# Linear attention, kv and M computed head by head on 32-column and 32x32 tiles of TensorE

## The chip, the cores and the metric

The kernel runs on one core of one Trainium2 chip. The metric is the device time of one execution in microseconds. The kernel before takes 298.92 us, the median of three runs (298.63 to 299.31).

## The reference

Two branches share one input x of 2048 rows by 640 columns and are mixed by a gate:

```python
qkv = (x @ wqkv).reshape(B, S, 3, H, Dh)      # H = 32 heads, Dh = 20
phi = lambda t: jnp.where(t > 0, t + 1, jnp.exp(t)) + 1e-6
pq, pk = phi(q), phi(k)
kv = einsum("bhsd,bhse->bhde", pk, v)          # per head 20 x 20
z = einsum("bhsd->bhd", pk)
o = (pq @ kv) / (pq . z + 1e-6)                # per head
b = o.reshape(B, S, D) @ wo
return g * a + (1 - g) * b                     # a: an SSM convolution of x; g: sigmoid of x . gate_w
```

Everything is float32.

## The kernel before

The k rows are made first, 128 at a time, and with them G = x^T phi(k), a 640 by 640 sum in PSUM (the long part of the program, until about 145 us). G is copied to SBUF as GT, in five blocks b of 128 rows. Since v = x Wv, a head's kv is a product of 20 columns of Wv with the same 20 columns of GT, summed over b. M is kv times wo, head by head, 640 by 640. The output is then phi(q), scaled by 1/den, times M. This last stage (fp, from about 200 us on) reads M as two float32r parts, a rounded high part and the remainder, Mh and Ml, and does three products for each float32 one (`mm3`, lines 105 to 108). kv and M are plain float32 products; the trace shows two matmuls for each of them. With a `tile_position` (row, column) a product uses only a part of the 128 by 128 array.

From 145 us on the order of the work is set by a list, `PLAN` (line 64): each word calls one function, which issues its instructions on all engines, and each engine runs its instructions in that order. `q` is one q block (15 matmuls of 512 columns, exponential and relu on ACT, the rest of phi and the accumulator of den on DVE), `z` the constants and the gate row, `kv`, `m` the products in question, `c` one convolution block, `d` den's two matmuls and the reciprocal, `ml` the reload of M, `n` the scaling of one q block, `y` a finished convolution block, `f` one output block.

The heads are taken in six groups of 120 columns (`GRP`, the last of 40), each in two parts of 60 columns, three heads. `kv_mm(pr)` does two groups: for each part and b a product 60 by 60 into PSUM (line 279), of which `bdm` (ones in three 20 by 20 blocks) keeps the blocks of the three heads (line 284). `m_mm(pr)` multiplies the two groups' kv with wo. Its four parts lie on the four 64x64 tiles of the array (line 297), in two halves of 320 columns. ACT then rounds each PSUM bank into Mgh (`hi`, line 100) and DVE subtracts it into Mgl (`lo`, line 103). Both are stored to DRAM (line 315), from where `m_load` (line 706) reads them in the order of rows that the last stage wants.

PSUM after 145 us is eight banks in three rings: m of two, f of three, q of three. A ring's next tile waits until the work on the one that it replaces is done. An insertion of M takes two tiles of m and two of f. SBUF tiles are rings too: `bufs` is their length, `st` and `wo` hold what was loaded, `m1` holds GT and later Mh, `m2` holds Wv and later Ml.

Of the kernel before, what the change touches and what calls it, by code (L numbers as in the profile page):

```python
# [30 lines left out]
F32 = mybir.dt.float32  # L31
# [17 lines left out]
GRP = [(i * 120, min(120, D - i * 120)) for i in range(6)]  # L49
HC = 60  # L50
# [14 lines left out]
q0 z kv0 kv1 kv2 q0 q0 m0 q0 c q0 m1  # L65
q1 d0 q1 m2 ml n0 q1 n0 n0 q1 n0 y q1 n0
# [8 lines left out]
def f32(ap):  # L75
    return ap.bitcast(F32)


def body(tc, i, outT):
# [19 lines left out]
    def hi(dst, src):  # L99
        act.activation(dst, src, AF.Copy)  # L100
# [9 lines left out]
    def col(tag, n=NB, dt=F32):  # L110
        return pc.tile([P, n], dt, tag=tag, name=tag)
# [27 lines left out]
    bdm = col("bdm", HC)  # L139
    kvz = [col(f"kvT{k}", P) for k in range(3)]  # L140
# [7 lines left out]
    gap = col("gap", 16)  # L148
# [3 lines left out]
    M_d = [dram.tile([D, D], F32, name=f"M_d{x}") for x in "hl"]  # L152
# [101 lines left out]
    kvs, wos = {}, {}  # L254


    def parts(gi):
        c0, n = GRP[gi]
        return [(r, c0 + o, min(HC, n - o)) for r, o in ((0, 0), (64, HC)) if o < n]

    def wo_load(gi):
        tag, nb = ("st", 3) if gi in (0, 1, 2) else ("wo", 2)
        w = wos[gi] = pw.tile([P, D + 2], F32, tag=tag, bufs=nb, name="wo")
        for r, c, n in parts(gi):
            m = min(64, D - c) if r == 0 else n
            sp.dma_start(w[r : r + m, :D], i["wo"][c : c + m, :])
# [3 lines left out]
    def out_row(gi, r):  # L270
        return r if gi % 2 == 0 else 64 - r

    def kv_mm(pr):
        p = pqp.tile([P, 512], F32, tag="f", bufs=3, name="kvps")
        kvT = kvs[pr] = kvz[pr]
        for k, gi in enumerate((2 * pr, 2 * pr + 1)):
            for b in range(NB):
                for r, c, n in parts(gi):
                    pe.matmul(p[r : r + n, k * 64 : k * 64 + n], Wv[:, b, c : c + n], GT[:, b, c : c + n],
                              start=(b == 0), stop=(b == NB - 1))  # L280
        for k, gi in enumerate((2 * pr, 2 * pr + 1)):
            for r, c, n in parts(gi):
                o = out_row(gi, r)
                dve.tensor_tensor(kvT[r : r + n, o : o + n], p[r : r + n, k * 64 : k * 64 + n], bdm[r : r + n, :n],
                                  op=OP.mult)

    def m_mm(pr):
        kvT = kvs.pop(pr)
        both = 2 * pr, 2 * pr + 1
        ps = {}  # L290
        for hf in range(2):
            for gi in both:
                ps[gi, hf] = mbank("mps") if hf == 0 else pqp.tile([P, 512], F32, tag="f", bufs=3, name="mps")
            for gi in both:
                for r, c, n in parts(gi):
                    o = out_row(gi, r)
                    pe.matmul(ps[gi, hf][o : o + 64, :320], kvT[r : r + n, o : o + 64],
                              wos[gi][r : r + n, hf * 320 : hf * 320 + 320], start=True, stop=True,
                              tile_position=(r, o))
        for gi in both:  # L300
            wos.pop(gi)
        if pr == 1:
            wo_load(NB)
        for gi in both:
            rows = slice(0 if len(parts(gi)) == 2 else out_row(gi, 0), P)
            h = pq.tile([P, D], F32R, tag="so", bufs=2, name="Mgh")
            l = pw.tile([P, D + 2], F32R, tag="st", bufs=3, name="Mgl")
            for hf in range(2):
                sl = slice(hf * 320, hf * 320 + 320)
                hi(h[rows, sl], ps[gi, hf][rows, :320])  # L310
                lo(l[rows, sl], ps[gi, hf][rows, :320], h[rows, sl])
            for v, to in ((h, M_d[0]), (l, M_d[1])):
                for r, c, m in parts(gi):
                    o = out_row(gi, r)
                    sp.dma_start(to[c : c + m, :], f32(v[o : o + m, :D]))
# [204 lines left out]
    for r in (0, 64):  # L520
        sp.dma_start(bdm[r : r + HC, :], i["bdm"][:HC, :HC])
# [18 lines left out]
    for T in range(1, NT):  # L540
# [56 lines left out]
        if T == NT - 1:  # L597
            wqA, wqB = w_tiles(3 * P, "wA", "wqA"), w_tiles(CB, "wB", "wqB")
            for c in WQ:
                wq_split(wqA, c, 0, 3)  # L600
            for c in WQ:
                wq_split(wqB, c, 3, NB)
                raw.pop(c)
            gates()
            for gi in range(NB):
                wo_load(gi)
# [17 lines left out]
    def mbank(name):  # L624
        return pqp.tile([P, 512], F32, tag="m", bufs=2, name=name)
# [73 lines left out]
    def m_load():  # L699

        for x, tag, src in zip("hl", ("m1", "m2"), M_d):
            w = pc.tile([P, NB, D], F32, tag=tag, name="M" + x)
            m[x] = w.bitcast(F32R)
            rows = src.rearrange("(h b i) c -> b h i c", b=NB, i=QI)
            for b in range(NB):
                sp.dma_start(w[:, b, :], rows[b])
# [29 lines left out]
    for w in PLAN.split():  # L736
# [12 lines left out]
        elif what == "kv":  # L749
            kv_mm(k)  # L750
        elif what == "m":
# [193 lines left out]
```

## Time and profile before

| | us |
|---|---|
| median of 3 runs (lowest, highest) | 298.92 (298.63, 299.31) |
| the profiled execution | 298.69 |
| its span | 296.9 |
| TensorE busy in the span | 291.7 |
| DVE, ACT, POOL busy | 228.6, 125.1, 47.0 |
| kv products, start to the next q matmul | 150.29 to 153.56 |
| the three insertions of M start at | 160.56, 168.82, 177.56 |
| loads of Mh and Ml are issued | 186.65 to 193.35 |
| first output product | 199.78 |

A row of the timeline gives the start, the duration of the merged instructions, the engine, the line, the operation, out<-in, partitions by elements and the count; what stands in brackets is the idle time before it and what ended it. PE rows are matmuls, PEld rows loads of weights. For matmuls the shape is rows times columns of the array, then the moving operand. Ends of matmuls are modelled, so a distance between starts is safer than a duration.

### The profile page before, as it was taken

The numbers are of one execution on the slowest core, as the hardware profiler recorded it, in microseconds if no ns is written. First come the engines' busy times: TensorE is split into PE (matmuls) and PEld (weight loads), VectorE is DVE, ScalarE is ACT, GpSimd is POOL, SyncE is SP. The second block draws the span as 40 slices with busy tenths as digits, with TensorE's granted clock in tenths as the row PEclk, the third lists the DMA queues.
The fourth block names the chain that finished last, engine by engine and source line by source line (L and its number), as shares of the span: only waits on it lengthen the run. The fifth ranks groups of instructions, "written<-read, shape, count | busy, mean of one in ns | idle before, by whom it ended". The sixth has DMA issues, their size and how long they took to land.

```text
span 296.9 us, 4579 instructions
## 1 busy us (share of the span) xinstructions
PE 291.7 (98%) x1627; PEld 254.3 (86%) x1627; DVE 228.6 (77%) x355; ACT 125.1 (42%) x262; POOL 47.0 (16%) x52
## 2 busy tenths in 40 slices
PE   8999999999999999999999999999999999999994
PEld 7998899999999999999887777888888888888884
DVE  2869987899999799955743769968683777787992
ACT  3555144653565545337624374562323233314100
POOL 3601760000000000000000000003313203232541
PEclk9999999999999999999999999999999999999999
DMA  6925477257767854280364563792416022426323
GB/s 171 330 69 184 132 242 232 86 200 234 235 152 256 249 168 156 82 256 1 88 174 138 164 203 106 231 329 79 141 35 186 29 71 71 142 73 182 125 85 111
DMA packets 28409, 46.00 MB, mean 155 GB/s; under 512 B 3771, under 2 KB 10827, under 8 KB 28383
## 3 DMA queue, kind: packets, MB, share of 16 engines
q1 hardware_dynamic: 28383, 45.66, 49.0%
q8 instruction: 15, 0.25, 0.3%
q14 instruction: 11, 0.09, 0.1%
HBM read 32.92 MB, written 12.72 MB: 154 GB/s over the span
## 4 chain that ended last, share of the span: by engine, by line
PE 96%; DMA 1%; SPq 0%; ACT 0%; DVE 0%; issue 0%
PE qp L106 8%; PE fp L107 8%; PE fp L108 8%; PE fp L106 8%; PE qp L107 8%; PE qp L108 8%; PE g L232 6%; PE g L231 6%; PE g L234 6%; PE k L108 6%; PE k L107 6%; PE k L106 6%; PE g L459 3%; PE r L247 2%; PE r L246 2%; PE r L245 2%
## 5 line engine op out<-in xcount | busy, mean ns | idle before, releaser
L444 POOL TENSOR_TENSOR yb<-yb,gb 128x512 f32<-128x512 f32 x20 | 28.3, 1417 | 217.8 <-DMA yb<-y_d 199.6
L108 PE MATMUL fp<-pTl,Mh 128*128 128x512 f32 (+1 forms) x105 | 39.8, 379 | 0.0
L107 PE MATMUL fp<-pTh,Ml 128*128 128x512 f32 (+1 forms) x105 | 39.8, 379 | 0.0
L106 PE MATMUL fp<-pTh,Mh 128*128 128x512 f32 (+1 forms) x105 | 39.8, 379 | 0.0
L232 PE MATMUL g<-ph,xl 128*128 128x512 f32 x80 | 31.4, 392 | 0.0
L231 PE MATMUL g<-ph,xh 128*128 128x512 f32 x80 | 31.3, 391 | 0.0
L652 DVE SCALAR_TENSOR_TENSOR qe<-qe,qr 128x512 f32<-128x512 f32 x20 | 14.3, 716 | 21.7 <-ACT qr L649 21.6
L100 ACT ACTIVATE pTh<-qe 128x512 fp32r<-128x512 f32 x20 | 12.6, 633 | 41.4 <-DVE qe L688 41.4
L210 DVE SCALAR_TENSOR_TENSOR e<-e,r 128x320 f32<-128x320 f32 x32 | 15.7, 496 | 13.2 <-ACT e L207 13.2
L106 PE MATMUL qp<-xTh,wqAh 128*128 128x512 f32 x60 | 23.8, 396 | 0.0
L648 ACT ACTIVATE qe<-qp 128x512 f32<-128x512 f32 x20 | 11.9, 595 | 28.0 <-PE qp L108 23.0
L204 ACT ACTIVATE e<-k 128x320 f32<-128x320 f32 x12 | 5.3, 438 | 43.4 <-PE k L108 43.4
L107 PE MATMUL qp<-xTh,wqAl 128*128 128x512 f32 x60 | 23.4, 390 | 0.0
L108 PE MATMUL qp<-xTl,wqAh 128*128 128x512 f32 x60 | 23.4, 389 | 0.0
L234 PE MATMUL g<-pl,xh 128*128 128x512 f32 x80 | 23.3, 389 | 0.0
L106 PEld LDWEIGHTS fp<-pTh,Mh 128*128 128x128 f32 x105 | 19.8, 188 | 3.8
L107 PEld LDWEIGHTS fp<-pTh,Ml 128*128 128x128 f32 x105 | 19.7, 188 | 3.8
L108 PEld LDWEIGHTS fp<-pTl,Mh 128*128 128x128 f32 x105 | 19.7, 188 | 3.7
L103 DVE TENSOR_TENSOR pTl<-qe,pTh 128x512 fp32r<-128x512 f32 x20 | 16.1, 817 | 6.8 <-ACT pTh L100 6.3
L424 DVE TENSOR_TENSOR_SCAN y<-y,cY,zero 128x512 f32<-128x512 f32 x16 | 20.5, 1278 | 0.8 <-ACT y L423 0.8
L108 PE MATMUL k<-wkBl,xTh 128*128 128x320 f32 x60 | 18.5, 309 | 0.0
L107 PE MATMUL k<-wkBh,xTl 128*128 128x320 f32 x60 | 18.5, 309 | 0.0
(171 smaller groups left out, 720.9 us busy)
## 6 DMA issues: line engine op xcount, KB each, us to landing
xraw<-in_x SPq DMA_DIRECT2D x16, 320.0 KB, 4.4
u<-in_xT SPq DMA_DIRECT2D x20, 256.0 KB, 5.7
out_T<-o SPq DMA_DIRECT2D x19, 256.0 KB, 2.6
y_d<-y SPq DMA_DIRECT2D x16, 256.0 KB, 2.4
yb<-y_d SPq DMA_DIRECT2D x16, 256.0 KB, 3.1
xTraw<-in_xTt SPq DMA_DIRECT2D x12, 320.0 KB, 4.5
Wv<-in_wv SPq DMA_DIRECT2D x5, 320.0 KB, 5.8
Mh<-M_dh SPq DMA_DIRECT2D x5, 320.0 KB, 4.5
```

What stands on the lines that cost most here:

```text
L100: act.activation(dst, src, AF.Copy)
L103: (eng or dve).tensor_tensor(dst, src, f32(h), op=OP.subtract)
L106: pe.matmul(out, ah, bh, start=start, stop=False)
L107: pe.matmul(out, al, bh, start=False, stop=False)
L108: pe.matmul(out, ah, bl, start=False, stop=stop)
L210: dve.scalar_tensor_tensor(e, e, 1.0, r[:, :n], op0=OP.min, op1=OP.add)
L231: pe.matmul(gps[b], xh[:, s], h[:, :512], start=t == 0, stop=False)
L232: pe.matmul(gps[b], xl[:, s], h[:, :512], start=False, stop=False)
L234: pe.matmul(gps[b], xh[:, b * P : b * P + P], l[:, :512], start=False, stop=t == NT - 1)
L424: dve.tensor_tensor_scan(y, y, zero.to_broadcast([P, 512]), cY[:, c], op0=OP.add, op1=OP.add)
L444: pool.tensor_tensor(ys[j], ys[j], gbs[j // NB], op=OP.mult)
L652: dve.scalar_tensor_tensor(e, e, 1.0, r, op0=OP.min, op1=OP.add)
```

## The change

The heads are taken one by one. Head 16 s + 4 r + c stands in set s (0 or 1), row r and column c of four. A kv product takes 32 columns of Wv (20 of the head, 12 that are not used) against the head's 20 columns of GT, on the tile (0, 32 r) of 128 rows by 32 columns; `kv_mm(s)` makes sixteen heads, 80 products. Two copies move the blocks to `kvT`; the mask `bdm` with its two loads is gone. `m_mm(n)` is set n/2 and half n mod 2 of M: sixteen products, each on its own 32x32 tile, one PSUM bank for each r. The 32 rows of a head keep their 12 rows of padding: M in DRAM has 1024 rows instead of 640, stored in half rows of 320 columns, by five stores for each insertion: four of 128 rows and one of 512. `m_load` leaves the padding out. The second set's wo is loaded into GT's place once kv is done. The list is changed: two kv words instead of three, directly followed as before by a q block, and four m words, after the q blocks 2, 3, 5 and 6, instead of three, after 3, 5 and 7.

```diff
 PLAN = """
-q0 z kv0 kv1 kv2 q0 q0 m0 q0 c q0 m1
-q1 d0 q1 m2 ml n0 q1 n0 n0 q1 n0 y q1 n0
+q0 z kv0 kv1 q0 m0 q0 m1 q0 c q0 m2
+q1 m3 d0 q1 ml n0 q1 n0 n0 q1 n0 y q1 n0
...
-    bdm = col("bdm", HC)
-    kvz = [col(f"kvT{k}", P) for k in range(3)]
+    kvz = [col(f"kvT{k}", P) for k in range(2)]
...
-    M_d = [dram.tile([D, D], F32, name=f"M_d{x}") for x in "hl"]
+    M_d = [dram.tile([32 * H, D], F32, name=f"M_d{x}") for x in "hl"]
...
+    def wo_load(s):
+        if s == 0:
+            v = [pw.tile([P, D + 2], F32, tag=t, bufs=n, name="wo") for t, n in (("st", 3), ("wo", 2)) for _ in range(2)]
+        else:
+            w = pc.tile([P, NB, D], F32, tag="m1", name="wo1")
+            v = [w[:, c, :] for c in range(4)]
+        wos[s] = v
+        wo = i["wo"]
+        for c in range(4):
+            row = (16 * s + c) * DH
+            n = 4 if row + 12 * DH + 32 <= D else 3
+            src = bass.AP(tensor=wo.tensor, offset=wo.offset + row * D, ap=[[4 * DH * D, n], [D, 32], [1, D]])
+            sp.dma_start(v[c][: n * 32, :D], src)
+            if n == 3:
+                sp.dma_start(v[c][96 : 96 + DH, :D], wo[row + 12 * DH : row + 13 * DH, :])
+
+    def kv_mm(s):
         p = pqp.tile([P, 512], F32, tag="f", bufs=3, name="kvps")
...
+        for c in range(4):
             for b in range(NB):
...
+                for r in range(4):
+                    h0 = (16 * s + 4 * r + c) * DH
+                    n = min(32, D - h0)
+                    pe.matmul(p[32 * r : 32 * r + n, 32 * c : 32 * c + DH], Wv[:, b, h0 : h0 + n],
+                              GT[:, b, h0 : h0 + DH], start=(b == 0), stop=(b == NB - 1), tile_position=(0, 32 * r))
+        src, dst = [v[:, :P].rearrange("p (c q) -> p c q", q=32)[:, :, :DH] for v in (p, kvz[s])]
+        for c, rows in ((slice(0, 3), P), (slice(3, 4), 96 + DH)):
+            dve.tensor_copy(dst[:rows, c, :], src[:rows, c, :])
+
+    Mg = {}
+
+    def m_mm(n):
+        s, hf = divmod(n, 2)
+        sl = slice(hf * 320, hf * 320 + 320)
+        ps = [mbank("mps") if r < 2 else pqp.tile([P, 512], F32, tag="f", bufs=3, name="mps") for r in range(4)]
+        for c in range(4):
+            for r in range(4):
+                pe.matmul(ps[r][32 * c : 32 * c + 32, :320], kvz[s][32 * r : 32 * r + DH, 32 * c : 32 * c + 32],
+                          wos[s][c][32 * r : 32 * r + DH, sl], start=True, stop=True, tile_position=(32 * r, 32 * c))
+        if hf == 0:
+            big = pc.tile([P, NB, D], F32R, tag="m2", name="Mg")
+            v = [pw.tile([P, D + 2], F32R, tag=t, bufs=nb, name="Mgs")
+                 for t, nb in ((("st", 3),) if s == 0 else (("st", 3), ("st", 3), ("wo", 2), ("wo", 2)))]
+            if s == 0:
+                v += [pq.tile([P, D], F32R, tag="so", bufs=2, name="Mgs") for _ in range(2)] + [big[:, 4, :]]
+            Mg[s] = big, v
+        big, v = Mg[s]
+        for r, p in enumerate(ps):
+            h, l = (big[:, r, sl], v[r][:, sl])[:: 1 - 2 * s]
+            hi(h, p[:, :320])
+            lo(l, p[:, :320], h)
+        for r in range(4):
+            row = 512 * s + P * r
+            sp.dma_start(M_d[1 - s][row : row + P, sl], f32(v[r][:, sl]))
+        rows = M_d[s][512 * s : 512 * s + 512, sl]
+        sp.dma_start(rows.rearrange("(r p) n -> p r n", p=P), f32(big[:, :4, sl]))
...
-            rows = src.rearrange("(h b i) c -> b h i c", b=NB, i=QI)
+            rows = src.rearrange("(h q) c -> h q c", q=32)
             for b in range(NB):
-                sp.dma_start(w[:, b, :], rows[b])
+                sp.dma_start(w[:, b, :], rows[:, b * QI : b * QI + QI, :])
...
         elif what == "kv":
             kv_mm(k)
+            if k == 1:
+                wo_load(1)
```

TensorE around the kv products, before (kvps is their PSUM tile, gp the gate row, qp a q block):

```order
L347 MATMUL cp<-zsl,bm 128x2
L326 MATMUL gp<-ident,g 16x128
L279 MATMUL kvps<-GT,Wv 60x60 x50
L279 MATMUL kvps<-GT,Wv 40x40 x5
L106 MATMUL qp<-xTh_131,wqAh 128x512
```

and now (the last head has no columns behind it, so its five products are 20 by 20):

```order
L342 MATMUL cp<-zsl,bm 128x2
L321 MATMUL gp<-ident,g 16x128
L278 MATMUL kvps<-GT,Wv 32x20 x143
L278 MATMUL kvps<-GT,Wv 20x20
L278 MATMUL kvps<-GT,Wv 32x20 x3
L278 MATMUL kvps<-GT,Wv 20x20
...
L104 MATMUL qp<-xTh_128,wqAh 128x512
```

160 products stand where 55 stood, in the same place.

TensorE between the sixth q block and den's products (dp), where the last insertion now is, with the engines whose semaphores each row waits for:

```order
L106 MATMUL qp<-xTl_462,wqAh 128x512
L292 MATMUL mps<-wo_1969,kvT_100 32x320 [waits DVE_49] x2
L292 MATMUL mps<-wo_1969,kvT_100 32x320
L292 MATMUL mps<-wo_1969,kvT_100 32x320 [waits DVE_49]
L292 MATMUL mps<-wo_1969,kvT_100 32x320 x12
L665 MATMUL dp<-acch,bm 128x512 [waits DVE_49]
```

Before, den's products followed the q block directly and the last insertion came one q block later. The first, second and fourth product of this insertion wait for DVE, and twelve stand behind.

DVE from the fourth q block to the reciprocal, before (Mgl is M's remainder, qe and acc are q blocks' work, y the convolution):

```order
L652 SCALAR_TENSOR_TENSOR qe<-qe,qr 128x512
L658 SCALAR_TENSOR_TENSOR acc<-qe,zc,acc 128x512
L424 SCALAR_TENSOR_TENSOR y<-y,cY,zero 128x512
L427 SCALAR_TENSOR_TENSOR y<-u,dsk,y 128x512
L652 SCALAR_TENSOR_TENSOR qe<-qe,qr 128x512
L658 SCALAR_TENSOR_TENSOR acc<-qe,zc,acc 128x512
L103 TENSOR_TENSOR accl<-acc,acch 128x512
L103 TENSOR_TENSOR Mgl<-mps,Mgh 128x320 x4
L652 SCALAR_TENSOR_TENSOR qe<-qe,qr 128x512
L677 RECIPROCAL d<-d 128x512
```

and now:

```order
L419 SCALAR_TENSOR_TENSOR y<-y,cY,zero 128x512
L422 SCALAR_TENSOR_TENSOR y<-u,dsk,y 128x512
L644 SCALAR_TENSOR_TENSOR qe<-qe,qr 128x512
L650 SCALAR_TENSOR_TENSOR acc<-qe,zc,acc 128x512
L101 TENSOR_TENSOR accl<-acc,acch 128x512
L101 TENSOR_TENSOR Mg<-mps,Mgs 128x320 x4
L644 SCALAR_TENSOR_TENSOR qe<-qe,qr 128x512
L101 TENSOR_TENSOR Mg<-mps,Mgs 128x320 x4
L669 RECIPROCAL d<-d 128x512
```

Four more subtractions, the last insertion's, stand ahead of the reciprocal; before they stood behind it.

More of the change, by code (lines that the diff above doesn't have):

```diff
@@ L48 @@
 CA, CB = 320, 320
-GRP = [(i * 120, min(120, D - i * 120)) for i in range(6)]
-HC = 60
 EPS = 1e-6
@@ L147, in body @@
     bm, zh = col("bm", P, F32R), col("zh", H)
-    gap = col("gap", 16)
+    gap = col("gap", 76)
     pool.memset(gap, 0.0)
@@ L251, in g_out @@
         (hi if eng is act else dve.tensor_copy)(GT[:, b, :512], src)
[L254 to L266, printed above, removed]
@@ L270, in out_row @@
-    def out_row(gi, r):
-        return r if gi % 2 == 0 else 64 - r
-    def kv_mm(pr):
+    wos = {}
+    def wo_load(s):
[13 more added lines that the diff above has]
+                sp.dma_start(v[c][96 : 96 + DH, :D], wo[row + 12 * DH : row + 13 * DH, :])
@@ L274, in kv_mm @@
+    def kv_mm(s):
         p = pqp.tile([P, 512], F32, tag="f", bufs=3, name="kvps")
-        kvT = kvs[pr] = kvz[pr]
-        for k, gi in enumerate((2 * pr, 2 * pr + 1)):
+        for c in range(4):
             for b in range(NB):
[L278 to L315, printed above, removed]
@@ L519, in body @@
     sp.dma_start(ident, i["ident"])
-    for r in (0, 64):
-        sp.dma_start(bdm[r : r + HC, :], i["bdm"][:HC, :HC])
     sp.dma_start(dtc, i["log_dt"])
@@ L604, in body @@
             gates()
-            for gi in range(NB):
-                wo_load(gi)
+            wo_load(0)
     g_rest(NT - 1)
```

## The prediction

> **What bounds the kernel now.** I read the page first, then the waits, then the timeline of TensorE around the work that the change touches.
>
> ```profile
> span 296.9 us, 4579 instructions
> PE 291.7 (98%) x1627; PEld 254.3 (86%) x1627; DVE 228.6 (77%) x355; ACT 125.1 (42%) x262; POOL 47.0 (16%) x52
> PE   8999999999999999999999999999999999999994
> PEclk9999999999999999999999999999999999999999
> PE 96%; DMA 1%; SPq 0%; ACT 0%; DVE 0%; issue 0%
> ...
> PEld mps L297 <- issue: 1.1, 3, 0.4
> PE k L131 <- POOL ones L122: 1.0, 1, 1.0
> ```
>
> TensorE is busy in every slice, the granted clock is full throughout, and the chain that ended last is TensorE for 96%. In the list of waits its longest are about 1 us. So what counts is TensorE time removed or added in the middle, and any new moment at which TensorE waits. The next rows show the kv products, the first insertion of M and the ordinary q matmuls.
>
> ```profile
> 149.72 0.39 PE L108 MATMUL qp<-xTl,wqAh 128*128 128x512 f32 x1
> ...
> 150.29 3.34 PE L279 MATMUL kvps<-GT,Wv 128*60 128x60 f32 x110
> 153.56 0.50 PE L106 MATMUL qp<-xTh,wqAh 128*128 128x512 f32 x1
> ...
> 159.56 0.39 PE L108 MATMUL qp<-xTl,wqAh 128*128 128x512 f32 x1
> ...
> 160.24 0.39 PE L108 MATMUL qp<-xTl,wqAh 128*128 128x512 f32 x1
> 160.56 1.31 PE L297 MATMUL mps<-wo,kvT 60*64 60x320 f32 x16
> 161.80 0.50 PE L106 MATMUL qp<-xTh,wqBh 128*128 128x512 f32 x1
> ...
> 162.37 0.39 PE L108 MATMUL qp<-xTl,wqBh 128*128 128x512 f32 x1
> ```
>
> An fp32 product stands as two matmuls in the trace (55 kv products, x110; 8 of M, x16). I call them pieces. The kv stage takes 153.56 - 150.29 = 3.27 us. Three q matmuls take 0.68 us (159.56 to 160.24), but 2.13 us with the insertion between them (160.24 to 162.37), so one insertion costs 1.45 us. The three insertions, of equal length below (the third holds fewer pieces), cost 4.35 us.
>
> ```profile
> 168.82 1.31 PE L297 MATMUL mps<-wo,kvT 60*64 60x320 f32 x16
> ...
> 177.56 1.30 PE L297 MATMUL mps<-wo,kvT 60*64 60x320 f32 x12
> ```
>
> The same timeline cut inside the first insertion, at 160.60 and at 161.10, shows how pieces overlap.
>
> ```profile
> 160.56 0.50 PE L297 MATMUL mps<-wo,kvT 60*64 60x320 f32 x4
> ...
> 160.56 0.77 PE L297 MATMUL mps<-wo,kvT 60*64 60x320 f32 x8
> ...
> L297 PE MATMUL mps<-wo,kvT x44: 429/429/480, 160.6 to 178.4; 60*64 60x320 f32 x40, 40*64 40x320 f32 x4
> ```
>
> Four pieces, one on each of the four 64x64 tiles, start within 0.50 - 0.48 = 0.02 us, that is 0.007 us apart. Each further wave of four adds 0.27 us. [...]
>
> **The kv part.** Before, two column groups work at once, on 60 columns: 110 pieces in 3.27 us, about 0.055 us for a pair. A line through 60 columns (0.055) and 320 (0.27) is 0.0055 us and 0.00083 us for each column. Loading weights costs about the same for each column: the ten zp pieces move 1 column each past 128 columns of weights and start the next group after 1.03 us, 0.103 each.
>
> ```profile
> 144.90 1.17 PE L337 MATMUL zp<-ones,zacc 128*128 128x1 f32 x10
> 145.93 0.74 PE L631 MATMUL tp<-ident,rem 128*128 128x128 f32 x5
> ```
>
> After, 160 products (320 pieces) lie in four column groups of 32 columns, with 20 moving columns. The weights are the longer side: 0.0055 + 32 x 0.00083 = 0.032 us for a wave, 80 waves, 2.56 us. Before, by the same line, it was 50 pairs x 0.055 plus ten 40-column pieces alone x 0.039 = 3.14 us. The kv term is -0.58 us. Bounds: pieces 0.007 us apart as at an insertion's start give 320 x 0.007 = 2.2 us (-0.9). The pace of the longest such run, 3.27/110 = 0.030 us a piece, gives 9.5 us (+6.4). I take the wave, since both 55 ns pairs and 270 ns waves followed it, and since a pair of pieces 7 ns apart leaves room for four in 32 ns.
>
> **The M part.** 64 products instead of 22, sixteen at once on 32x32 tiles, in four insertions. An insertion has 32 pieces in two waves of sixteen. Against four waves it saves 2 x 0.27 = 0.54 us, and the last of sixteen starts 12 x 0.007 = 0.08 us later than the last of four. One insertion then costs 1.45 - 0.54 + 0.08 = 0.99 us, four cost 3.96 us. The M term is -0.39 us. Bounds: without the later start 4 x 0.91 (-0.7). If sixteen tiles overlap no better than four, eight waves each, 4 x 2.53 (+5.8). I take two waves, because waves of three (x12 in the same 1.30 us) and of four behave alike.
>
> **A new wait.** Each insertion writes four PSUM banks, two of a ring of two (m) and two of a ring of three (f). Insertion n's rows 0, 1 and 3 reuse the banks of insertion n-1's rows 0, 1 and 2, which are free once DVE's subtraction of that row is done; DVE is in program order. Between insertions 0 and 1, and again between 2 and 3, there is now a single q block. The two old insertions that stand where insertions 1 and 2 will stand (after the third and after the fifth q block) show when the subtractions end.
>
> ```profile
> 163.18 1.68 DVE L103 TENSOR_TENSOR Mgl<-mps,Mgh 128x320 fp32r<-128x320 f32 x4
> ...
> 168.04 1.28 DVE L424 TENSOR_TENSOR_SCAN y<-y,cY,zero 128x512 f32<-128x512 f32 x1
> 169.36 0.75 DVE L427 SCALAR_TENSOR_TENSOR y<-u,dsk,y 128x512 f32<-128x512 f32 x1
> ...
> 170.77 0.75 DVE L658 SCALAR_TENSOR_TENSOR acc<-qe,zc,acc 128x512 f32<-128x512 f32 x1
> 172.28 0.69 DVE L103 TENSOR_TENSOR accl<-acc,acch 128x512 fp32r<-128x512 f32 x1 [0.76 <-ACT acch L100]
> 172.89 1.68 DVE L103 TENSOR_TENSOR Mgl<-mps,Mgh 128x320 fp32r<-128x320 f32 x4
> ...
> 173.35 0.39 PE L108 MATMUL qp<-xTl,wqAh 128*128 128x512 f32 x1
> ...
> L103 DVE TENSOR_TENSOR Mgl<-mps,Mgh 128x320 fp32r<-128x320 f32 x10 | 4.2, 483 | 0.0
> ```
>
> After an ordinary q block, the four subtractions start 163.18 - 160.56 = 2.62 us behind the insertion's start and step by (1.68 - 0.48)/3 = 0.40; the third ends at 2.62 + 0.80 + 0.48 = 3.90 us. Insertion 1 comes one q block later. Without a wait it would start, counted from its predecessor, at the 0.78 us that two waves take, plus a q block (from 170.06, below, to 173.35 is 3.29) and the 0.32 us lead (160.24 to 160.56): 4.39 us. That is 0.5 us to spare, so insertion 1 doesn't wait.
>
> After the fifth q block it is otherwise. The convolution's scan and product, the accumulator and its split stand ahead of the subtractions. Put on the old trace's clock, insertion 3 would start at 173.35 + 0.32 - 0.46 = 173.21. The third subtraction ends at 172.89 + 0.80 + 0.48 = 174.17. Row 3's first product is the fourth issued, so the other twelve stand behind it: a wait of about 1.0 us. What is queued behind on TensorE is den's two matmuls and the next q block, and the whole rest shifts. Bounds: 0 (nothing waits) and 1.1 us. I take 0.97.
>
> ```profile
> 170.06 0.50 PE L106 MATMUL qp<-xTh,wqAh 128*128 128x512 f32 x1
> ```
>
> [...]
>
> **What costs nothing.** Four more copies on ACT and four more subtractions on DVE (2 us each), less eleven kv multiplications (the 2.58 us below) for four copies: DVE and ACT are 22.7 and 15.4 us busy of 33 there. M's stores carry padded rows, 5.2 MB instead of 3.3, under a DMA share of 0.45; if they landed late, the first product of M waits.
>
> ```profile
> 152.14 2.58 DVE L284 TENSOR_TENSOR kvT<-kvps,bdm 60x60 f32<-60x60 f32 x11
> ...
> 154.00:187.00 33.00, 33.00 (x172) 24.98 (x171) 22.71 (x37) 15.35 (x32) 0.00 (x0) 1.00 0.45 143
> ...
> 182.41 1.81 DVE L103 TENSOR_TENSOR Mgl<-mps,Mgh 128x320 fp32r<-128x320 f32 x4
> ...
> 199.78 0.39 PE L106 MATMUL fp<-pTh,Mh 128*128 128x512 f32 x1
> ```
>
> Now the last subtractions end at 184.2, behind the reciprocal. After, insertion 3's stand ahead of it and end at about 178, so the stores and the reload of M start some 6 us earlier against its first use at 199.78. Two tiny loads (bdm) and one memset fewer lie beside the start.
>
> **Sum.** -0.58 - 0.39 + 0.97 = 0.0 us. The profiled execution took 298.69 us around its span of 296.9; the median shown, 298.92, is 0.23 above. I predict 298.9 us.
>
> **The rivals.**
>
> *TensorE is not supplied fast enough (slower).* The kv stage becomes 320 weight loads and 320 matmuls in 2.56 us, 4.0 ns each. The longest dense run before had 220 in 3.27 us, 14.9 ns each, and was limited by its columns; the 3.4 ns of four pieces starting together may be only what was queued. From 4.9 ns on the change is slower by over 0.2% (640 x 0.0049 = 3.1 us). At 9 ns, between both rows, kv is 5.8 us, 3.2 more: 302.1 us. For it: no row shows more than sixteen pieces at such a pace. Against it: the starts 7 ns apart. [...]
>
> *Four column streams don't run at full pace (slower).* Before, two groups of columns read at once, now four. If only two are fed, waves double: kv +2.6, M four waves again, 4 x 0.54 = +2.2: 303.7 us. That the sixteen don't overlap at all belongs here: the change wouldn't do what it says. Nothing shows it; the overlap of two and of four tiles was full.
>
> *The wait at insertion 3 doesn't come (faster).* If DVE reaches the subtractions 1 us earlier, or banks are released otherwise, 297.9 us; with the 0.007 us pace for kv too, 297.6. Against it: scan, product and accumulator stand ahead of them as before.
>
> **Chances.** Forecast 0.50, supply 0.22, streams 0.10, no wait 0.18. A measurement here tells 0.2%, 0.6 us, from no change. Forecast: 0.43 same, 0.04 faster, 0.03 slower. No wait: 0.16 faster, 0.02 same. Both slower rivals: slower. Faster 0.20, same 0.45, slower 0.35. The range is 297.7 to 302.3 us: it takes in the faster rival and supply up to 9 ns. The forecast's own range is 298.2 to 299.4.
>
> **What would show it.** kvps: x320 within 2.6 us, not over 3.2. Each mps insertion: x32, the next q matmul about 0.8 us after its start in the first three. Before or within the fourth, about 1 us in which TensorE waits for DVE's subtraction (L101 there). fp must start without a wait. A kv stage over 3.2 us, or a fourth insertion without a wait, breaks the forecast.

## The result, and the profile after

The change is slower: 315.80 us median of 5 runs (314.96 to 316.21) against 298.79 us for the kernel before on the same chip, a ratio of 1.0567 with a 95% interval from 1.0553 to 1.0581. The forecast was 298.9 us, its range ended at 302.3. The profiled execution took 315.56 us around a span of 313.8.

The page of the change, its head, the slices of TensorE and of its clock, and the shares of the chain that ended last:

```profile
span 313.8 us, 5158 instructions
PE   8999999999999999999699689999999999999993
PEclk9999999999999999999879859999999999999998
PE 89%; DMA 7%; issue 1%; SPq 1%; ACT 1%; DVE 0%; DVEq 0%
```

Where every slice of TensorE between the first and the last stood at 9, and every slice of its clock, there are now two dips in both, TensorE's at slices 20 and 23 to 24, the clock's at 20 to 21 and 23 to 24 (a slice is 7.8 us). The chain holds 7% of transfers and 1% of "issue", which is time in which an engine waited for nothing that the profile shows. The timeline of TensorE through both dips (start, us from the first start to the last end, line, operation, shapes, count, then the idle time ahead of the row and what ended it):

```profile
150.32 2.25 PE L278 MATMUL kvps<-GT,Wv 128*32 128x20 f32 x242
155.31 1.26 PE L278 MATMUL kvps<-GT,Wv 128*32 128x20 f32 x78 [2.73 <-issue]
156.50 0.80 PE L104 MATMUL qp<-xTh,wqAh 128*128 128x512 f32 x1
157.09 0.63 PE L105 MATMUL qp<-xTh,wqAl 128*128 128x512 f32 x1
157.52 0.63 PE L106 MATMUL qp<-xTl,wqAh 128*128 128x512 f32 x1
...
162.47 0.82 PE L292 MATMUL mps<-wo,kvT 20*32 20x320 f32 x32
163.22 0.50 PE L104 MATMUL qp<-xTh,wqAh 128*128 128x512 f32 x1
...
166.85 0.82 PE L292 MATMUL mps<-wo,kvT 20*32 20x320 f32 x32
167.60 0.50 PE L104 MATMUL qp<-xTh,wqBh 128*128 128x512 f32 x1
...
174.63 0.74 PE L292 MATMUL mps<-wo,kvT 20*32 20x320 f32 x8
175.53 0.74 PE L292 MATMUL mps<-wo,kvT 20*32 20x320 f32 x8 [0.17 <-DMA wo<-in_wo]
178.72 1.29 PE L292 MATMUL mps<-wo,kvT 20*32 20x320 f32 x8 [2.44 <-DMA wo<-in_wo]
181.90 1.45 PE L292 MATMUL mps<-wo,kvT 20*32 20x320 f32 x8 [1.89 <-DMA wo<-in_wo]
183.28 0.80 PE L104 MATMUL qp<-xTh,wqAh 128*128 128x512 f32 x1
183.87 0.63 PE L105 MATMUL qp<-xTh,wqAl 128*128 128x512 f32 x1
...
189.47 1.39 PE L292 MATMUL mps<-wo,kvT 20*32 20x320 f32 x32
190.79 0.50 PE L665 MATMUL dp<-acch,bm 128*128 128x512 f32 x1
```

242 pieces of kv run at the predicted pace, then TensorE stands still for 2.73 us with nothing to wait for. The q matmuls behind that start 0.43 us apart (157.09 to 157.52) where 0.23 us is usual: the granted clock is 0.50 there. Insertions 0 and 1 take 0.75 us each (162.47 to 163.22). Insertion 2 takes 8.65 us, since three of its four tiles of wo come one after the other at 3.2 us; and again a q block at half clock follows. All 16.9 us are accounted for by rows of the two traces:

| stretch | before, us | after, us | more |
|---|---|---|---|
| up to the first kv product | 150.29 | 150.32 | 0.03 |
| kv, to the next q matmul | 3.27 | 6.18 | 2.91 |
| from there to the first product with M (fp) | 46.22 | 59.13 | 12.91 |
| of that: q block behind kv, 5.97, against 3.63 undisturbed (163.22 to 166.85) | | | 2.34 |
| of that: insertion 2, 8.65 against 0.75 | | | 7.90 |
| of that: q block behind insertion 2, 6.19 against 3.63 | | | 2.56 |
| of that: insertion 3, 1.32 against 0.75 | | | 0.57 |
| of that: the rest, four insertions for three | | | -0.46 |
| first product with M to the end of the last matmul | 93.17 | 93.17 | 0.00 |
| from there to the end of the span | 3.96 | 4.99 | 1.02 |

Five of the waits between 150 and 200 us (engine, waiting tile and line, releaser; total, times, longest):

```profile
DVE Mg L101 <- DMA M_dh<-Mg: 9.9, 1, 9.9
PEld mps L292 <- DMA wo<-in_wo: 6.8, 3, 3.0
PE mps L292 <- DMA wo<-in_wo: 4.5, 3, 2.4
PEld kvps L278 <- issue: 2.8, 1, 2.8
PE kvps L278 <- issue: 2.7, 1, 2.7
```

The longest single wait is DVE's, 9.9 us, for a store of the first set's Mg. TensorE doesn't show it, since it is itself held up by wo and then slow. SP's queue tells how these belong together:

```profile
144.27 2.76 SPq L267 DMA_DIRECT2D wo<-in_wo  x4
...
152.27 0.34 SPq L324 DMA_DIRECT2D g_d<-gr  x1
161.74 1.76 SPq L402 DMA_DIRECT2D gb<-g_d  x4
163.62 2.84 SPq L267 DMA_DIRECT2D wo<-in_wo  x4
166.51 5.57 SPq L269 DMA_DIRECT2D wo<-in_wo  x1
...
175.55 0.38 SPq L310 DMA_DIRECT2D M_dh<-Mg  x1
178.74 3.98 SPq L308 DMA_DIRECT2D M_dl<-Mgs  x3
```

The first set of wo goes out at 144.27; the 8 KB of g_d behind it take from 152.27 to 161.7 to land, and gb and the second set stand in line behind that. The stores of M at 175.55 and 178.74 leave 0.02 us after TensorE gets a tile of wo (175.53, 178.72): their semaphores are those of the tiles' transfers, eight issues earlier, and SP, in order, waits for them. What makes the transfers slow shows where nothing else moves:

```profile
169.00:172.00 3.00, 3.00 (x15) 2.49 (x14) 2.15 (x5) 1.03 (x4) 0.00 (x0) 1.00 0.26 96
```

The last two columns are the DMA share and GB/s: 0.26 of sixteen engines is 4.2, at 96 GB/s. A tile of 327,680 bytes then takes 3.4 us as an estimate; insertion 2 gets its tiles 3.2 us apart. The read of line 267, of three dimensions, has 4 as its outermost count. That this count sets how many engines are busy was the author's guess; this stretch shows no more than that the two agree, 4.2 and 4.

### The profile page after: what moved, and what is told of

It is laid out like the page before. It is cut to its first block, busy times and chain, and to the rows that moved or that the text cites. A ratio compares the mean times of both kernels' runs of the same rounds, so it can differ in the third digit from the quotient of the medians.

```text
span 313.8 us, 5158 instructions
## 1 busy us (share of the span) xinstructions
PE 300.3 (96%) x1921; PEld 258.3 (82%) x1921; DVE 230.1 (73%) x352; ACT 126.5 (40%) x266; POOL 46.3 (15%) x51
## 4 chain that ended last, share of the span: by engine, by line
PE 89%; DMA 7%; issue 1%; SPq 1%; ACT 1%; DVE 0%; DVEq 0%
PE fp L106 7%; PE fp L105 7%; PE fp L104 7%; PE qp L104 7%; PE qp L105 7%; PE qp L106 7%; PE g L229 6%; PE g L228 6%; PE g L231 6%; PE k L106 6%; PE k L105 6%; PE k L104 6%; DMA wo<-in_wo 5%; PE g L454 3%; PE r L244 1%; PE r L243 1%
## 5 line engine op out<-in xcount | busy, mean ns | idle before, releaser
L104 PE MATMUL qp<-xTh,wqAh 128*128 128x512 f32 x60 | 26.0, 433 | 0.0
L105 PE MATMUL qp<-xTh,wqAl 128*128 128x512 f32 x60 | 25.3, 421 | 0.0
L106 PE MATMUL qp<-xTl,wqAh 128*128 128x512 f32 x60 | 25.1, 419 | 0.0
```

Source lines behind the costliest of these rows:

```text
L104: pe.matmul(out, ah, bh, start=start, stop=False)
L105: pe.matmul(out, al, bh, start=False, stop=False)
L106: pe.matmul(out, ah, bl, start=False, stop=stop)
```

## Experiments: the form of wo's transfers, the order of kv

Theory after the two traces: two separate losses, each followed by half clock. In kv, TensorE's instructions run out; at insertion 2, wo is late because of the form of its transfers. Rivals: the small products are slow as such, or bring the half clock; wo is late because SP issues it late.

**wo32**: both sets of wo in pieces of 32 rows.

```diff
-            src = bass.AP(tensor=wo.tensor, offset=wo.offset + row * D, ap=[[4 * DH * D, n], [D, 32], [1, D]])
-            sp.dma_start(v[c][: n * 32, :D], src)
+            for r in range(4):
+                h0 = row + 4 * r * DH
+                n = min(32, D - h0)
+                sp.dma_start(v[c][32 * r : 32 * r + n, :D], wo[h0 : h0 + n, :])
```

> Both sets of wo are read in pieces of 32 rows instead of one transfer of four strips per tile; nothing else differs from the changed kernel. Theory (a transfer whose outermost step counts 4 keeps about four packets in flight, so a tile takes 3.2 us, and every later transfer of SP queues behind it): m2 finds its wo there, the 7.8 us of its wait go, the half-speed q block behind it goes too (2.6 us), and DVE's 9.9 us wait for the store goes; the gap in kv and the half-speed block behind that stay. 315.6 - 10.4 = 305.2 us, between 304 and 307. Rival (the loads are late because SP issues them late, behind gb and behind the release of GT, and the form of the transfer doesn't matter): m2 still waits over 3 us, and the time is 310 us or more.

Measured: 306.98 us (302.84 to 307.80, 4 runs), ratio 1.0229 (1.0155 to 1.0303). Insertion 2 takes 0.75 us, as the theory said, and the median lies within the expected range, near its upper end. From 146 to 152 us, where the first set's loads run, the DMA share is 0.57 at 156 GB/s; in the change it is 0.31 at 111. How much came back is not clear of the spread: 8.8 us by the medians, 10.1 by the ratios, where 10.4 were expected. The trace (of an execution of 307.8 us) shows insertion 3 on TensorE, and DVE ahead of it:

```profile
172.45 0.82 PE L291 MATMUL mps<-wo,kvT 20*32 20x320 f32 x32
...
180.12 1.68 PE L291 MATMUL mps<-wo,kvT 20*32 20x320 f32 x32 [3.23 <-DVE Mg L101]
```

```profile
179.57 1.68 DVE L101 TENSOR_TENSOR Mg<-mps,Mgs 128x320 fp32r<-128x320 f32 x4 [2.97 <-DMA M_dh<-Mg]
```

At least in this execution, the slowest of the four, DVE's wait for the first set's store, hidden before, now reaches TensorE: the remainders of the second set go into the tile (tag m2) from which that store still reads.

**wo32_set1**: the same for the second set alone.

```diff
+            if s == 1:
+                for r in range(4):
...
+                    sp.dma_start(v[c][32 * r : 32 * r + n, :D], wo[h0 : h0 + n, :])
+                continue
```

> Only the second set of wo is read in pieces of 32 rows; the first is as in the changed kernel and still holds up g_d and gb until 161.7 us, so the second set is issued no earlier than before, from 163.6 us on. Theory (the form of the second set's transfers is what m2 waits for): sixteen issues of about 0.45 us end at 171 us, all landed by 173 us, m2 starts at 174.6 without a wait: 305.2 us as with both sets, between 304 and 307. Rival (the late issue is what counts): m2 waits 3 us or more, 309 us or more.

Measured: 312.77 us, ratio 1.0465 (1.0421 to 1.0509). Insertion 2 went through in 1.21 us although the set was issued no earlier, so the form of the transfers is what it waited for. The time that the theory expected from it did not come: SP issues the stores of M behind the sixteen loads, and insertion 3 waits 4.95 us for DVE, which waits 5.2 us for the first set's store (M_dh<-Mg). Each cure moved the wait to the next transfer in SP's line.

**kv_apart**: one q block between kv0 and kv1.

```diff
-q0 z kv0 kv1 q0 m0 q0 m1 q0 c q0 m2
+q0 z kv0 q0 kv1 m0 q0 m1 q0 c q0 m2
```

> Only the order differs from the changed kernel: one q block stands between kv0 and kv1. Theory (PE's instructions run dry in kv: about 545 rows of PE and its weight loads are used up before a further 16 KB block is there): neither kv0 nor kv1 has a gap over 1 us, and the q blocks behind them run at the full clock, so PE is some 5 us earlier at m1. The time hardly shows it, since the landing of the second set of wo does not move: m2 waits some 5 us longer, and the total stays at 315.6, between 313 and 317. Rival (the small products cannot be started faster whatever stands between, or the gap has to do with the change from one set to the other): a gap of about 2.7 us remains in kv1 or between the sets, and the clock falls behind it.

Measured: 315.79 us, ratio 1.0563 (1.0539 to 1.0588): nothing gained in time, as expected, and no gap in kv, as the theory had it. Where the time went was a surprise:

```profile
150.54 1.54 PE L278 MATMUL kvps<-GT,Wv 128*32 128x20 f32 x160
...
155.66 1.53 PE L278 MATMUL kvps<-GT,Wv 128*32 128x20 f32 x160
157.12 1.45 PE L292 MATMUL mps<-wo,kvT 20*32 20x320 f32 x24
161.04 1.29 PE L292 MATMUL mps<-wo,kvT 20*32 20x320 f32 x8 [2.48 <-DMA wo<-in_wo]
162.26 0.80 PE L104 MATMUL qp<-xTh,wqAh 128*128 128x512 f32 x1
162.86 0.63 PE L105 MATMUL qp<-xTh,wqAl 128*128 128x512 f32 x1
```

Insertion 0 now waits, for the first set of wo, which lands at 161.0. In the change it seemed free of waits only because the gap and the half clock had delayed it to 162.47. And the half clock comes here behind a wait for a transfer, with both kv parts run through at full clock.

**wo32_apart**: both edits.

> Both edits together. Theory (two separate losses, each followed by a stretch at half clock): they add, 305.2 - 2.7 - 2.3 = 300.2 us, between 299 and 301.5; the granted clock is 1.0 nearly everywhere; what is left over the kernel before is the wait of insertion 3 for its banks and the tail. Rival (the half clock comes from the small square products themselves and not from PE standing still): a stretch at half clock stays behind kv or behind an insertion of M, and the time is 302.5 or more.

Measured: 308.61 us, ratio 1.0322 (1.0300 to 1.0345), 8.4 us more than expected and no better than wo32 alone. TensorE is earlier, but the first set's stores are not: DVE waits 5.7 us for one of them (the store M_dh<-Mg issued at 176.08 lands at 180.36, and DVE's subtractions start at 180.54), and insertion 3 waits 5.37 us for DVE. There is also a pause of 0.88 us marked "issue" in the q block behind insertion 0, without a half clock behind it. The two losses don't add; a third one, the store, takes up what they give.

## Experiments: what runs out in kv

**kv_three**: the change, with every kv product issued three times.

```diff
-        for c in range(4):
-            for b in range(NB):
+        for b, c in [(b, c) for _ in range(3) for c in range(4) for b in range(NB)]:
```

> The changed kernel with every product of kv issued three times over (the same sums again; 960 products in place of 320, so some 1920 rows of PE and its weight loads in place of 640). Theory (PE's instructions arrive in blocks of 16 KB, some 250 rows, and the next comes only about 3.3 us after the one before): after the first 450 to 550 rows in kv a gap comes at each block, the stage takes (1920 - 500) / 250 = 5.7 blocks at 3.3 us and 2.3 us before them, about 21 us, where 240 waves at 0.032 us would take 7.7 us. Rival (one late block, and then the supply keeps up): one gap of about 2.7 us, 10.4 us in all.

Measured: one execution, 326.92 us; the kv stage took 26.9 us (150.46 to 177.39), more than the 21 expected and far from the rival's 10.4. TensorE, kv only:

```profile
150.46 2.23 PE L277 MATMUL kvps<-GT,Wv 128*32 128x20 f32 x242
155.36 1.91 PE L277 MATMUL kvps<-GT,Wv 128*32 128x20 f32 x128 [2.67 <-issue]
159.09 1.91 PE L277 MATMUL kvps<-GT,Wv 128*32 128x20 f32 x128 [1.81 <-issue]
...
168.46 1.92 PE L277 MATMUL kvps<-GT,Wv 128*32 128x20 f32 x128 [3.73 <-issue]
...
176.19 1.27 PE L277 MATMUL kvps<-GT,Wv 128*32 128x20 f32 x78 [2.09 <-issue]
```

After the first pause the pieces come in lots of exactly 128, with their weight loads 256 instructions, one lot per 3.7 to 4.0 us (once 5.64). Count TensorE's rows in the trace from the program's start, beginning with 0 (matmuls, weight loads and a few others, 27 of them before the change's first pause), and the first row behind every pause named "issue" that ends in kv or in a q block is:

```
change, wo32, wo32_set1, smooth_burst        2241
late_wo1, wo32_apart                         2497
kv_three   2241  2497  2753  3009  3265  3521
```

All lie 256 apart: these are walls at fixed places of the program. The list of transfers has packets of 16,384 bytes on a queue for instructions (q8, 17 packets in the change), one for each 256 rows of TensorE, which makes 64 bytes for an instruction as an estimate. In the change row 1985 started at 151.28, a packet at 153.08, and row 2241 at 155.31, 4.0 us after the wall before. In all twelve pauses it is the same: the packet starts 0.9 to 3.2 us behind a wall, and the first row behind the next wall starts 2.2 to 2.9 us after the packet, read here as no further block being there yet. From wall to wall this took 3.2 to 4.1 us, and once 5.6; the pauses took 0.88 us (wo32_apart) to 3.73 us (kv_three). Where the 256 rows themselves took 4.7 us or more there was no pause. Without a pause kv would issue its 640 in less than 3 us. So 256 instructions in under some 4 us ran TensorE dry in these seven versions; late_few, below, is an exception.

**late_wo1**: the 32-row loads, kv0 and kv1 two q blocks apart, the second set's loads behind insertion 1's stores, insertions 2 and 3 later.

```diff
+q0 z kv0 q0 m0 q0 kv1 m1 q0 c q0
+q1 d0 q1 m2 n0 q1 m3 ml n0 n0 q1 n0 y q1 n0
...
             m_mm(k)
+            if k == 1:
+                wo_load(1)
```

> The 32-row loads of wo; kv0 and kv1 two q blocks apart; the loads of the second set moved behind insertion 1 in SP's order, so the stores of the first set go ahead of them; insertion 2 two q blocks later, insertion 3 and the loads of Mh and Ml with it. Theory (three separate losses: the instructions running dry in kv, the four-strip transfers, and the store that holds DVE because SP issued it behind the second set): no wait of PE above 1 us is left between 150 and 200 us and the clock stays at 1.0, though all the small square products are still there. By the parts measured without waits (kv 2 x 1.47 in place of 3.27, M 4 x 0.75 in place of 3.72, a tail up to 1.0 longer) 298.8 us, between 297.5 and 301; the upper end if Mh or Ml come late at the first product with M. Rival (the small products themselves bring the half clock, or the insertions wait for banks whatever the order): a stretch at half clock or a wait over 1 us stays at an insertion, 302 or more.

Measured: 306.98 us (305.20 to 308.79), ratio 1.0277 (1.0244 to 1.0310), 8 us more than expected. The store's wait is gone, but 320 instructions of kv1 ran dry all the same:

```profile
159.79 1.43 PE L277 MATMUL kvps<-GT,Wv 128*32 128x20 f32 x146
163.12 0.41 PE L277 MATMUL kvps<-GT,Wv 128*32 128x20 f32 x14 [1.90 <-issue]
164.60 2.55 PE L291 MATMUL mps<-wo,kvT 20*32 20x320 f32 x32 [1.07 <-DVE Mgs L101]
167.09 0.80 PE L104 MATMUL qp<-xTh,wqBh 128*128 128x512 f32 x1
```

Here kv1 began at row 2204, just ahead of wall 2241, and reached 2497 3.2 us behind that wall. In kv_apart the same 320 began at 2107 and ended before 2497. So distance alone doesn't help; what matters is how many instructions lie between two walls and how long they take. This was not understood when the expectation was written.

**late_few**: the order of late_wo1 with the change's own loads.

> The order of the run before this one, with the loads of wo in the changed kernel's form (four strips in one transfer). Theory (the form of the transfer is a loss of its own that a better order does not heal): insertion 0 waits for the first set until about 161 us, some 5 us; the second set, issued from about 165 us on at 3.2 us a tile, is there at about 180, and insertion 2 waits some 4 us or more; 306 us or more, with two stretches at half clock. Rival (the order alone was at fault): within 1 us of the run before this one.

Measured: 319.30 us, ratio 1.0687 (1.0670 to 1.0705), 12.3 us more than late_wo1. Insertions 0 and 2 both wait for wo, as the theory had it. But kv1, which crosses both walls at the same rows as in late_wo1, runs through without a pause:

```profile
168.04 1.53 PE L278 MATMUL kvps<-GT,Wv 128*32 128x20 f32 x160
```

Its rows go from wall 2241 to wall 2497 in 1.08 us. The packet had started at 166.88, 1.3 us ahead of the first of the two walls; in late_wo1 it started 1.0 us behind it. The second wall comes 2.4 us after the packet, as late as a row behind a pause does elsewhere. So 256 instructions in 4 us are no limit by themselves; by these thirteen cases what decides is when the next packet comes. Why it came earlier here is not shown; the q block ahead ran at half clock until 166.95.

## Experiments: all losses taken away

**smooth**: each set of kv in two parts that may stand apart; the first set of wo in 32-row pieces, the second in four transfers whose outermost count is 20.

```diff
+q0 z kv0 kv1 q0 kv2 q0 m0 kv3 q0 m1 q0 c
+q1 m2 d0 q1 m3 ml n0 q1 n0 n0 q1 n0 y q1 n0
...
+        if s == 1:
+            for r in range(4):
+                row = (16 + 4 * r) * DH
+                src = bass.AP(tensor=wo.tensor, offset=wo.offset + row * D, ap=[[D, DH], [DH * D, 4], [1, D]])
+                sp.dma_start(w[32 * r : 32 * r + DH, :4, :], src)
+            return
...
+        for c in (0, 1) if half == 0 else (2, 3):
```

> kv in four parts (each set in two, columns c = 0, 1 and c = 2, 3): both parts of the first set together, the two of the second each behind a q block of its own; the first set of wo in 32-row pieces, the second in four transfers whose outermost step counts 20 (20 rows of the four column blocks, one transfer for each strip); the second set's loads stand in SP's order behind the stores of insertion 0; insertion 2 behind the sixth q block and insertion 3 behind the seventh, as the kernel before has its third insertion. Theory (PE's blocks of instructions hold about 255 rows, and a burst runs dry only if over 255 rows follow a block's boundary within some 4 us; here a q block of 3.4 us always lies between): no wait of PE above 1 us from 150 to 200 us, clock 1.0 throughout, 298.9 - 0.3 (kv) - 0.7 (M) + 0.5 (tail) = 298.4 us, between 297.5 and 299.7. Rival (the many small instructions cost time wherever they stand): a gap of 1.3 us or more with a half-speed stretch behind it stays at one of the parts, 301 or more.

Measured: 302.38 us, ratio 1.0101 (1.0074 to 1.0128). kv no longer pauses, and yet the time is 4.0 us above the one expected: insertion 2 took 3.4 us, since the second set landed at 175.9 behind the stores of insertion 0, and part of a q block ran at half clock behind it.

**smooth_few**: the order of smooth with the change's loads.

> The order of the run before this one (kv in parts, later insertions), with wo read in the changed kernel's form, four strips in one transfer. Theory (each tile takes 3.2 us in this form, whatever the order): the first set lands at about 161 us and holds insertion 0 some 2 us; gb and the second set follow it, so insertion 2 at about 174 waits some 3 us more and a half-speed block follows; 304 us, between 302 and 309. Rival (with a good order the form is hidden): within 1 us of the run before this one.

Measured: 313.51 us, ratio 1.0486 (1.0457 to 1.0515): 11.1 us more than smooth, beyond the upper end expected. Insertion 2:

```profile
174.49 0.74 PE L299 MATMUL mps<-wo,kvT 20*32 20x320 f32 x8 [1.05 <-DMA wo<-in_wo]
177.83 1.29 PE L299 MATMUL mps<-wo,kvT 20*32 20x320 f32 x8 [2.60 <-DMA wo<-in_wo]
182.00 1.29 PE L299 MATMUL mps<-wo,kvT 20*32 20x320 f32 x8 [2.88 <-DMA wo<-in_wo]
183.80 1.48 PE L299 MATMUL mps<-wo,kvT 20*32 20x320 f32 x8 [0.51 <-DMA wo<-in_wo]
```

Only the loads of wo differ between the two kernels, so their form alone costs 11 us in this order, with the half clock that follows it.

**smooth_burst** and **best2** differ from each other by kv's place alone, all in one or in parts between q blocks; in both the second set's loads go ahead of insertion 0's stores.

```diff
-q0 z kv0 kv1 kv2 kv3 q0 q0 m0 q0 m1 q0 c
+q0 z kv0 kv1 q0 kv2 q0 kv3 m0 q0 m1 q0 c
 q1 m2 d0 q1 m3 ml n0 q1 n0 n0 q1 n0 y q1 n0
```

> As the first run of this call but for the place of kv: its four parts stand together again, 320 products in a row, then two q blocks and insertion 0. Theory (the burst alone costs the gap of 2.7 us and up to 2.3 us at half clock behind it, and nothing downstream hides it any more): 298.4 + 5.0 = 303.4 us, between 302 and 304.5. Rival (the gap is covered by a wait that would come anyway): within 1 us of the first run.

> As the run in which all of kv stood together and the rest was mended, with nothing changed but that kv stands in its parts between q blocks (the first set together, the second in two). Against that run this tells the price of the burst alone: theory 2.9 us for the gap and 2.0 us for the half clock behind it, so 304.4 - 4.9 = 299.5 us, between 298.5 and 300.5; insertion 3 still waits about 1 us for its banks. Rival (the burst's price is partly hidden, or the parts pay it in small gaps): 301 us or more.

Measured: 304.42 us, ratio 1.0148 (1.0115 to 1.0181), for the burst (one of its four runs took 1655.84 us, which nothing here explains; without it the median is 304.19), and 300.42 us, ratio 1.0057 (1.0032 to 1.0082), in parts. The two were timed on different chips: the burst costs 2.7 us by the ratios to the kernel before and 3.8 by the medians, where 4.9 were expected. Its pause in kv is 2.79 us; the parts pay for their extra interruptions of the q blocks.

**best1**: insertion 2 moved directly behind the fifth q block, two q blocks ahead of insertion 3.

```diff
+q0 z kv0 kv1 q0 kv2 q0 kv3 m0 q0 m1 q0 c m2
+q1 d0 q1 m3 ml n0 q1 n0 n0 q1 n0 y q1 n0
```

> As the run in which kv stood in four parts apart, but with the last part of kv ahead of insertion 0, so that the second set's four loads go ahead of the stores of insertion 0 on SP, and with insertion 2 directly behind the fifth q block, two q blocks and the sums for d ahead of insertion 3. Theory (the second set of wo came 2.6 us late behind those stores and the half clock behind it cost 1.6 us; the rest of the loss was at insertion 3): no wait over 1 us at any insertion, clock 1.0: 302.4 - 4.2 = 298.2 us, between 297.3 and 299.5. Rival (there is one more loss that the waits hid): 300 us or more, with a new wait at insertion 3 or at the first product with M.

Measured: 299.33 us of 12 runs, ratio 1.0022 (1.0006 to 1.0039). Insertion 2 takes 1.83 us there, as part of its wo comes late. Every slice of the clock is back at full:

```profile
PEclk9999999999999999999999999999999999999999
```

**best3**: insertion 2 one q block later, insertion 3 two behind it, the loads of Mh and Ml one later.

```diff
-q0 z kv0 kv1 q0 kv2 q0 kv3 m0 q0 m1 q0 c m2
-q1 d0 q1 m3 ml n0 q1 n0 n0 q1 n0 y q1 n0
+q0 z kv0 kv1 q0 kv2 q0 kv3 m0 q0 m1 q0 c
+q1 m2 d0 q1 n0 q1 m3 ml n0 n0 q1 n0 y q1 n0
```

> As the version at 299.3 us, but insertion 2 behind the sixth q block (its wo has 3.4 us more) and insertion 3 two q blocks behind it, with the loads of Mh and Ml one q block later for that. Theory (what is left over is the 0.7 us of wo and the 0.3 us at insertion 2; M and kv without waits are 0.5 and 0.7 us cheaper than before, the tail 0.5 us dearer): 298.3 us, between 297.6 and 299.0, no wait over 0.5 us at M. Rival (the later loads of Mh and Ml hold up the first product with M): a wait of 1 to 3 us there, 299.5 to 301.5.

Measured: 299.34 us, ratio 1.0005 (0.9993 to 1.0018), no difference that can be measured. No insertion waits; the first fp block takes 3.96 us instead of 3.43, a small part of the rival's late Ml.

**best4**: best2 with the convolution's step c behind insertion 2.

```diff
+q0 z kv0 kv1 q0 kv2 q0 kv3 m0 q0 m1 q0
+q1 m2 c d0 q1 m3 ml n0 q1 n0 n0 q1 n0 y q1 n0
```

> As the version at 300.4 us, whose insertion 3 waited 1.03 us for its banks because the work of c stood ahead of insertion 2's evictions on ACT and DVE; here c stands behind insertion 2. Theory (the bank wait comes from the late evictions and not from the four banks as such): insertion 3 takes 0.75 to 1.0 us instead of 1.78, 299.6 us, between 298.8 and 300.2. Rival (insertion 3 one q block behind insertion 2 waits for its banks in any case, about 1 us, as the prediction had it): 300.4 again.

Measured: 299.63 us, ratio 1.0015 (0.9998 to 1.0031). Insertion 3 in best2 and in best4:

```profile
178.18 1.85 PE L304 MATMUL mps<-wo,kvT 20*32 20x320 f32 x32
```

```profile
178.38 1.61 PE L304 MATMUL mps<-wo,kvT 20*32 20x320 f32 x32 [0.39 <-DVE Mg L101]
```

To the next q matmul it is 1.78 and 1.54 us, where 0.75 needs no wait. Moving c took 0.24 us off, not the whole wait, so the theory there holds for a quarter of it. Two q blocks between the insertions (best1, best3) take it away.

No version was faster than the kernel before.

## Why the prediction was wrong, step by step

*The kv part, "I take the wave".* The pace was right: 60 waves start within 2.07 us (0.034 us a wave, 8.6 ns a piece; 0.032 us a wave was predicted). The step failed in taking that pace for all 80 waves. The change's kv took 6.18 us instead of the 2.7 that 3.27 - 0.58 gives. Without a pause, as two runs of 160 pieces in kv_apart, it takes 1.47 + 1.46 us, 0.34 less than before.

*The rival "TensorE is not supplied fast enough"* was the right kind of cause with a chance of 0.22, and its price was too low. It supposed a slower uniform pace, decided from 4.9 ns an instruction. 484 instructions ran at 4.3 ns; what ended was the stock of instructions. Such an end could not be read off a kernel whose kv had 220 instructions in 3.27 us.

*The M part.* Measured as the prediction did, from the q matmul ahead of insertion 1 (166.53) to the third behind it (168.18), less 0.68 us, an insertion costs 0.97 us; 0.99 was predicted. Four cost 0.47 us less than three did before; 0.39 was predicted. The rival of four column streams is out.

*The new wait at insertion 3, 0.97 us.* In the change 0.57 us, as the q block ahead of it ran at half clock. At full clock 1.03 us (best2) and 0.79 us (best4). The term holds; the convolution ahead of the subtractions explains only 0.24 us of it.

*"What costs nothing".* This is the step that cost most. It priced the copies, the subtractions and M's stores, and left out the loads of wo, which the change writes in a new form. They were 11.1 us in the pair smooth_few and smooth, and 7.90 us of standing still in the change. The sentence on late stores named the first product with M as the one that would wait; the stores held DVE instead, through the tile that they read from.

*No wait at insertions 0 and 1.* For insertion 1 this held: it takes 0.75 us in the change (166.85 to 167.60) and in best2 (165.39 to 166.14). Insertion 0 had none only for the reason that kv was late: with kv run through and the change's loads, it waited until 161.0 for the first set (kv_apart).

*The clock.* It had no term, since the kernel before never stood still. In the traces each long pause was followed by about a q block at half clock, 4.9 us in the change's ledger. It need not come each time: one of smooth_burst's runs had a mean granted clock of 0.999 and took 303.03 us, where 0.990 and 0.991 went with 304.65 and 304.19. The 0.88 us pause of wo32_apart and the 0.32 us wait of best1 were not. The shortest single pause with half clock behind it was 1.90 us (late_wo1), and in smooth two waits of 0.50 and 0.67 us within insertion 2 were enough. The small products alone don't bring it: best1 runs all of them at full clock. Ahead of the program's end the granted clock stood at half for 3.41 us or a whole multiple of it in every run that shows a half clock (6.83 and 10.24 us in the change). What decides whether it comes is not shown.

*The sum.* With the stalls gone, the terms kv and M are a gain of about 0.8 us, and yet best3 stands level with the kernel before. Two parts were not in the sum: from the last matmul to the end it takes 4.5 us in the mended versions instead of 3.96, and each further interruption of the q blocks costs 0.23 us (one q block between small products takes 3.63 us in the change, 163.22 to 166.85, two in a row 7.03, 167.60 to 174.63). In best3 the first fp block adds 0.53 us. What lengthens the end was not tried and stays open.

## What to carry to other kernels

Count instructions before splitting matmuls into small ones: 256 of TensorE's instructions (weight loads too) in less than about 4 us ran it dry in seven versions here and in one did not, so spread small products between long ones. Price every transfer that an edit rewrites, by its access pattern (the form of wo's loads alone cost 11.1 us between smooth_few and smooth), and follow what stands behind it in the issuing queue. A wait can hide the next: after a cure, look at which transfer or buffer ends last now, before adding up gains.

## What was not expected of the hardware

TensorE's instructions came in blocks of 256 (lots of 128 pieces with their weight loads in kv_three); where it ran dry, the first row of the next block started 2.2 to 2.9 us after its packet and 3.2 to 4.1 us (once 5.6) after the wall before. A transfer with 4 as its outermost count moved 96 GB/s at a DMA share of 0.26. TensorE's clock halved after a pause of 1.90 us (late_wo1), and half clock lasted 3.41 us or a whole multiple of it (6.83 and 10.24 us in the change).
